# A second product by 49 multiplications, with part of its operands kept in HBM

## The chip, the core and the metric

The kernel runs on one core of a Trainium2 chip. The metric is the device time of one execution in microseconds (us). Before the change it is 684.05 us, the median of three runs from 683.75 to 684.24. The profile covers one execution of its own, with a span of 683.1 us.

## What is computed

A recurrent attention ("retention") feeds a two-layer block with a sigmoid gate. All values are fp32 (the two weight matrices arrive as float64 bits and are narrowed in the kernel).

```python
# q, k, v: (4, 8, 768, 64); w_in: (512, 2048); w_out: (2048, 512)
for t in range(S):
    state = gamma * state + k[t] (outer) v[t]        # per batch and head, 64 x 64
    y[t]  = scale * q[t] @ state
x = y, as rows of 8 heads x 64 = (3072, 512)
h = x @ w_in                                         # the first product
g = h / (1 + exp(-1.702 * h))
out = g @ w_out                                      # the second product
```

## The kernel before

The 3072 rows are worked in six blocks m = 0..5 of 512. Attention runs in chunks of 128 steps, four to a block and ahead of the products, so that the attention of block m + 1 lies inside the second product of block m. From block 2 on, both products use a seven-product scheme: the operands are seen as 2 x 2 quarters, and seven products of sums of quarters, added in the right way, give the four quarters of the result. In blocks 0 and 1 only the second product does so.

The matmuls are in the order in which the program gives them; the other engines' instructions are put in order by a scheduler when the program is compiled, and each engine, and each engine's queue of transfers, then works strictly in that order.

The loads of one attention chunk. Later chunks fetch q and k as 16 small pieces each, in the arrangement that VectorE's 32 x 32 transposes need:

```python
for name, src in (("q", q), ("k", k)):
    t = two.tile([P, HP, P // C4, C4], F32, name=name + "_sq")        # two buffers
    for r0 in range(0, P, C4):
        for n in range(P // C4):
            tc.keep_in_program_order(sp.dma_start(t[r0:r0 + C4, :, n], ...))     # 16 KB each
...
def turn(j):                                       # j: the chunk
    for t, name in ((QT[j], "q"), (KT[j], "k")):
        tc.keep_in_program_order(dve.transpose(..., QKV.pop((name, j))...))
    if 2 * CB <= j < NCH - 2:
        load(j + 2, "qk")

def step(j, f=None):                               # scores of chunk j, outputs of chunk f = j - 1
    attend(j, f)                                   # TensorE
    masked(j); decay(j)                            # VectorE; GpSimd (kd)
    ... by_state(f), output(f), aged(f), updated(f)   # VectorE and GpSimd; output writes X
    load(j + 1, "v")                               # kn and v, SyncE
```

The first product of blocks 2 to 5, for a quarter `d` of the hidden columns:

```python
def up(d):
    def product(acc, sa, sb, start, stop):
        for u in range(2):
            for c in range(2):
                pe.matmul(acc[:, u, :], W1[:, 2 * d + u, sa, c, :], X[:, sb, c, :], ...)   # 128 x 256
    ...                                            # seven products; VectorE adds, ScalarE copies and gates
    hidden(a[1], x)                                # the last of four gated quarters of G
```

The second product (quarter sums of G are made by `sums_g`, of W2 by `sums_w2` in block 0):

```python
def part(key, sa, sb, new, last, d, then):
    ...
    for p in range(2 * d, 2 * d + 2):
        for n in range(2):
            pe.matmul(p0[:, n, :], g1(m, p, sa)[:, n * P:(n + 1) * P], W2[:, sb, p, :], ...)   # 128 x 256
    if d == NP // 2 - 1:
        then(p0)
P_ = [("x", 0, 0, ...), ("y0", 1, 2, ...), ("y1", 3, 1, ...), ("x", 0, 5, ...),
      ("y2", 3, 4, ...), ("x", 2, 6, ...), ("x2", 1, 3, ...)]        # seven products, 4 units each
```

The blocks:

```python
for m in range(NB):
    between = ... chunks((m + 1) * CB + 1, (m + 2) * CB)      # turn, step, turn, step, ...
    if m > 1:
        for d in range(NP // 2):
            up(d)
    for n, unit in enumerate(down(m)):             # 28 units
        unit()
        if m == 0 ...: sums_w2, sums_w2_t3
        if m == 1 and n % 8 == 3: sums_w1(n // 4)
        if between and n % 3 == 2:
            between.pop(0)()
            if m and not between:
                sums_x()                           # GpSimd: quarter sums of X for the next first product
```

W1 and W2 lie in SBUF with their seven quarter forms, `W1[P, 8, 7, 2, 128]` and `W2[P, 7, 8, 256]`, both for the whole execution.

Of the kernel before, what the change touches and what calls it, by code (L numbers as in the profile page):

```python
# [9 lines left out]
F32 = mybir.dt.float32  # L10
U32 = mybir.dt.uint32
AF = mybir.ActivationFunctionType
ALU = mybir.AluOpType
P = 128
# [14 lines left out]
def kernel(  # L29
# [29 lines left out]
    pe, act, dve, pool, sp = nc.tensor, nc.scalar, nc.vector, nc.gpsimd, nc.sync  # L59
    ctx.enter_context(tc.manual_schedule(engines={mybir.EngineType.PE}))  # L60

    B, H, S, D = q.shape
# [3 lines left out]
    NC = S // D  # L66
    NCH = B // 2 * NC
    CB = 4
    BT = CB * P
    TH = BT // 2  # L70
    NB = NCH // CB
    NFF = DFF // P
    NP = NFF // 2
    C4 = 32
    EH = DM // 2
    assert 2 * D == P and HP * P == DM and NC % CB == 0 and B % 2 == 0 and DM == 512 and NFF == 16

    const = ctx.enter_context(tc.tile_pool(name="const", bufs=1))
    one = ctx.enter_context(tc.tile_pool(name="one", bufs=1))
    two = ctx.enter_context(tc.tile_pool(name="two", bufs=2))  # L80
    ps_a = ctx.enter_context(tc.tile_pool(name="ps_a", bufs=1, space=bass.MemoryType.PSUM))
    ps = ctx.enter_context(tc.tile_pool(name="ps", bufs=2, space=bass.MemoryType.PSUM))

# [1 line left out]

    W1 = const.tile([P, NP, 7, 2, P], F32, name="W1")
    W2 = const.tile([P, 7, NP, EH], F32, name="W2")

    X = const.tile([P, 7, 2, TH], F32, name="X")

    G = const.tile([P, NP, 4, TH], F32, name="G")
# [8 lines left out]
    mask = const.tile([P, 2, HP, D], F32, name="mask")  # L102
    state = [const.tile([P, 2, HP, D], F32, name=f"state{i}") for i in range(2)]


    ordered = [True]

    def pin(i):
        return tc.keep_in_program_order(i) if ordered[0] else i
# [47 lines left out]
    def raw(i, n=1):  # L157
        x = RAWS[i // 2 % 3]
        return x[:, i % 2 * 1024:(i % 2 + n) * 1024]
# [5 lines left out]
    class Narrow:  # L165
# [4 lines left out]
        def __init__(self, i):  # L170
            n, p, h = (1 if i < 2 else 2), i // 2 % NP, i % 2

            if i < 2:
                m = W1[:, 1, 2 * h:2 * h + 2].rearrange("p s c f -> p (s c f)")
                w = W1[:, 0, h:4:2].rearrange("p ab c f -> p c ab f")
            elif i < NFF:
                m = W1[:, p, 0:4].rearrange("p s c f -> p (s c f)")
                w = W1[:, p, 0:4].rearrange("p (ab h) c f -> p (h c) ab f", ab=2)
            else:
                m = w = W2[:, 0:4, p]  # L180
            x = raw(i, n).rearrange("p (n two) -> p n two", two=2)
            self.lo, self.hi, self.m, self.w, self.i = x[:, :, 0], x[:, :, 1], m, w, i
            if i >= NFF:
                self.lo, self.hi = [t.rearrange("p (s e) -> p s e", s=4) for t in (self.lo, self.hi)]
            self.mu = m.bitcast(U32)
# [148 lines left out]
    def step(j, f=None):  # L334
        attend(j, f)
        if j is not None:
            masked(j)
            if j > 2 * CB:
                decay(j)
        if f is not None:  # L340
            c = f % NC
            if c == 0:
                updated(f)
            else:
                by_state(f)
            output(f)
            if 0 < c < NC - 1:
                aged(f)
                updated(f)
        if j is not None and 2 * CB < j < NCH - 1:  # L350
            load(j + 1, "v")


    def hidden(g, h):

        for g, i in g if isinstance(g, list) else [(g, slice(0, 2))]:
            pin(act.activation(g, h[:, i], AF.Gelu_apprx_sigmoid))  # L357

    def g(m, p, s):

        if m:
            return G[:, p:p + 2, s, :]
        if s < 3:
            return W1[:, p:p + 2, 4 + s].rearrange("p a c f -> p a (c f)")
        return X[:, 4 + p // 2] if p < 6 else G0

    def g1(m, p, s):
        return g(m, p // 2 * 2, s)[:, p % 2]

    def up0(th, p, tag):  # L370

        h = ps.tile([P, 2, TH], F32, name="ph", tag=tag)
        for ab in range(2):
            for c in range(4):
                w = W1[:, p, 2 * ab + c // 2, c % 2, :]
                pe.matmul(h[:, ab], w, X[:, 2 * th + c // 2, c % 2, :], start=(ab == 0 and c == 0), stop=(c == 3),  # L376
                          skip_group_check=True)
        if th == 0:
            return W1[:, p, 4:6].rearrange("p s c f -> p (s c f)"), h
        return [(g1(0, p, 2 + i), i) for i in range(2)], h  # L380

    def up1(f):

        p, ab = divmod(f, 2)
        h = ps.tile([P, 2, TH], F32, name="ph", tag="xy"[f % 2])
        for c in range(4):
            w = W1[:, p, 2 * ab + c // 2, c % 2, :]
            pe.matmul(h, w, X1[:, c // 2:4:2, c % 2, :], start=(c == 0), stop=(c == 3))  # L388
        return G[:, p, ab:4:2, :], h


    def sums_w1(p):
        w = [W1[:, p:p + 2, s] for s in range(7)]
        pool.tensor_add(w[4], w[2], w[3])
        pool.tensor_sub(w[6], w[0], w[2])
        pool.tensor_sub(w[5], w[4], w[0])
        pool.tensor_sub(w[2], w[1], w[5])

    def sums_x():
        pool.tensor_sub(X[:, 4], X[:, 2], X[:, 0])  # L400
        pool.tensor_sub(X[:, 6], X[:, 3], X[:, 2])
        pool.tensor_sub(X[:, 5], X[:, 3], X[:, 4])
        pool.tensor_sub(X[:, 2], X[:, 1], X[:, 5])
# [17 lines left out]

    def up(d):

        def product(acc, sa, sb, start, stop):
            for u in range(2):
                for c in range(2):
                    pe.matmul(acc[:, u, :], W1[:, 2 * d + u, sa, c, :], X[:, sb, c, :],  # L427
                              start=(start and u == 0 and c == 0), stop=(stop and c == 1), skip_group_check=True)

        a = [G[:, 2 * d:2 * d + 2, s, :] for s in range(4)]  # L430
        x = ps.tile([P, 2, TH], F32, name="px", tag="x")
        product(x, 0, 0, True, False)
        p1 = one.tile([P, 2, TH], F32, name="p1", tag="s1")
        act.activation(p1, x, AF.Copy)
        y = ps.tile([P, 2, TH], F32, name="py1", tag="y")
        product(y, 1, 1, True, True)
        dve.tensor_add(a[0], y, p1)  # L437
        hidden(a[0], a[0])
        product(x, 5, 5, False, False)
        u = one.tile([P, 2, TH], F32, name="u", tag="s2")  # L440
        act.activation(u, x, AF.Copy)
        z = ps.tile([P, 2, TH], F32, name="py2", tag="y")
        product(z, 4, 4, True, True)
        t = one.tile([P, 2, TH], F32, name="t", tag="s1")
        dve.tensor_add(t, z, u)  # L445
        product(x, 6, 6, False, False)
        vv = one.tile([P, 2, TH], F32, name="vv", tag="s3")
        act.activation(vv, x, AF.Copy)
        y = ps.tile([P, 2, TH], F32, name="py3", tag="y")
        product(y, 2, 3, True, True)  # L450
        dve.tensor_add(a[3], z, vv)
        hidden(a[3], a[3])
        dve.tensor_add(a[2], y, t)
        hidden(a[2], a[2])
        product(x, 3, 2, False, True)
        hidden(a[1], x)

    def down(m):

# [69 lines left out]
    first = const.tile([P, 1], F32, name="first")  # L529
    idle = ps.tile([P, 4 * P], F32, name="idle", tag="x")  # L530
    works, products = {}, {}
# [62 lines left out]
    for name, i in [("0a", 0), ("0b", 1)] + [(str(p), 2 * p) for p in range(1, NFF)]:  # L594
        n = Narrow(i)
# [40 lines left out]
    def chunks(first, last):  # L636

        return [s for j in range(first, last + 1)
                for s in (lambda j=j: turn(j), lambda j=j: step(j, j - 1))]

    for m in range(NB):
        between = []
        if m == 0:
            between = [lambda: turn(2 * CB), lambda: step(2 * CB), lambda: None, lambda: None, lambda: turn(2 * CB + 1)]
        elif m == 1:
            between = [lambda: (decay(2 * CB), load(2 * CB + 1, "v"))] + chunks(2 * CB + 1, 3 * CB)[1:]
        elif 1 < m < NB - 2:
            between = chunks((m + 1) * CB + 1, (m + 2) * CB)
        elif m == NB - 2:
            between = chunks((m + 1) * CB + 1, NCH - 1) + [lambda: step(None, NCH - 1)]  # L650
        if m > 1:
            for d in range(NP // 2):
                up(d)
        for n, unit in enumerate(down(m)):
            unit()
            if m == 0 and n < NP and n % 2:
                sums_w2(n - 1)
            if m == 0 and NP <= n < 3 * NP // 2:
                sums_w2_t3(2 * (n - NP))
            if m == 1 and n % 8 == 3:  # L660
                sums_w1(n // 4)
            if between and n % 3 == 2:
                between.pop(0)()
                if m and not between:
                    sums_x()


# [44 lines left out]
```

## Time and profile before

| quantity | value |
|---|---|
| time, median of 3 | 684.05 us |
| span of the profile | 683.1 us |
| TensorE, matmuls (PE) | 671.5 us busy |
| TensorE, weight loads (PEld) | 559.3 us |
| VectorE (DVE) | 306.0 us |
| ScalarE (ACT) | 151.0 us |
| GpSimd (POOL) | 124.9 us |
| moved by transfers | 46.54 MB |
| q and k pieces after the first chunks | 512 transfers of 16 KB, issued by SyncE (SP) |
| granted TensorE clock | 1.0 |

How the profile is read. Times are microseconds from the span's start. PE holds the matmuls and PEld the weight loads of TensorE; both overlap, and a matmul's end is modelled, so a group's mean duration is longer than the distance between two starts. `L495` is a line of the kernel; `out<-in` names tiles without buffer numbers. In a group's row, the busy time and mean duration in ns stand behind the first bar, and behind the second the engine's idle time ahead of these instructions with what ended it. SPq is SyncE's queue of transfers: its rows in the timeline show how long *issuing* takes. The time from issue to landing is listed apart, as a median for each kind of transfer.

The matmuls' lines are L376 (`up0`) and L388 (`up1`) in blocks 0 and 1, L427 (`up`) from block 2 on, L495 (`part`) and L480 (last part of block 5). Attention is at L265, L275, L284 and L290, VectorE's transposes at L235, the q and k pieces at L140, kn and v at L126.

### The profile page before, as it was taken

The numbers are of one execution on the slowest core, as the hardware profiler recorded it, in microseconds if no ns is written. First come the engines' busy times: TensorE is split into PE (matmuls) and PEld (weight loads), VectorE is DVE, ScalarE is ACT, GpSimd is POOL, SyncE is SP. The second block draws the span as 40 slices with busy tenths as digits, with TensorE's granted clock in tenths as the row PEclk, the third lists the DMA queues.
The fourth block names the chain that finished last, engine by engine and source line by source line (L and its number), as shares of the span: only waits on it lengthen the run. The fifth ranks groups of instructions, "written<-read, shape, count | busy, mean of one in ns | idle before, by whom it ended". The sixth has DMA issues, their size and how long they took to land.

```text
span 683.1 us, 13807 instructions
## 1 busy us (share of the span) xinstructions
PE 671.5 (98%) x5830; PEld 559.3 (82%) x5830; DVE 306.0 (45%) x410; ACT 151.0 (22%) x301; POOL 124.9 (18%) x116
## 2 busy tenths in 40 slices
PE   7899999999999999999999999999999999999997
PEld 4788854747888888888888888888888888888886
DVE  3789881869710842221652222563222372222241
ACT  4675423321000001332000332000333000233000
POOL 3000000000467414000334100245100243000020
PEclk9999999999999999999999999999999999999999
DMA  8887641332222223301333310323310210000001
GB/s 188 215 227 222 173 141 59 123 84 35 47 33 67 59 46 88 69 6 19 72 58 76 67 23 13 72 44 78 74 35 8 59 32 32 16 0 1 16 0 46
DMA packets 140334, 46.54 MB, mean 68 GB/s; under 512 B 131825, under 2 KB 132849, under 8 KB 140273
## 3 DMA queue, kind: packets, MB, share of 16 engines
q1 hardware_dynamic: 136352, 39.10, 24.8%
q0 software_dynamic: 1760, 5.26, 2.0%
q10 hardware_dynamic: 2160, 1.31, 0.6%
q8 instruction: 45, 0.74, 0.4%
q14 instruction: 17, 0.13, 0.1%
HBM read 39.33 MB, written 6.29 MB: 67 GB/s over the span
## 4 chain that ended last, share of the span: by engine, by line
PE 87%; DVE 5%; SPq 3%; DMA 3%; issue 1%; POOL 0%; ACT 0%; ACTq 0%; DVEq 0%
PE pd L495 37%; PE px L427 16%; PE py L427 12%; PE ph L376 8%; PE ph L388 5%; SPq L140 3%; PE pt L232 2%; PE pa L265 2%; PE py L290 2%; PE py L284 1%; PE pa L275 1%; DMA whole<-in_col_decay_dram 1%; PE pd L480 1%; DMA q_in<-in_q_dram 1%; DMA W<-in_moe_w_out_dram 1%; DVE G L417 1%
## 5 line engine op out<-in xcount | busy, mean ns | idle before, releaser
L495 PE MATMUL pd<-W,G 128*128 128x256 f32 x1088 | 240.5, 381 | 0.4 <-DVE G L418 0.3
L495 PEld LDWEIGHTS pd<-W,G 128*128 128x128 f32 x1088 | 205.2, 190 | 29.4 <-DVE G L418 1.2
L427 PE MATMUL px<-X,W 128*128 128x256 f32 x512 | 119.0, 379 | 0.0
L427 PEld LDWEIGHTS px<-X,W 128*128 128x128 f32 x512 | 97.3, 190 | 13.2
L427 PE MATMUL py<-X,W 128*128 128x256 f32 x384 | 90.7, 379 | 0.0
L427 PEld LDWEIGHTS py<-X,W 128*128 128x128 f32 x384 | 73.0, 190 | 9.9
L376 PE MATMUL ph<-X,W 128*128 128x256 f32 x256 | 57.6, 382 | 0.3 <-DVE X L312 0.3
L388 PE MATMUL ph<-W,W 128*128 128x512 f32 x128 | 55.6, 592 | 0.0
L376 PEld LDWEIGHTS ph<-X,W 128*128 128x128 f32 x256 | 48.1, 190 | 8.6 <-issue 1.6
L256 POOL TENSOR_TENSOR kd<-kn_in,cold 128x512 f32<-128x512 f32 x14 | 16.3, 1167 | 199.0 <-PE pa L275 111.9
L388 PEld LDWEIGHTS ph<-W,W 128*128 128x128 f32 x128 | 24.3, 190 | 28.9 <-issue 28.7
L419 POOL TENSOR_TENSOR G<-G 128x512 f32<-128x512 f32 x20 | 28.9, 1451 | 92.9 <-DVE G L418 91.1
L357 ACT ACTIVATE G<-G 128x512 f32<-128x512 f32 x48 | 30.2, 630 | 48.5 <-DVE G L437 29.9
L437 DVE TENSOR_TENSOR G<-py,p 128x512 f32<-128x512 f32 x16 | 11.1, 692 | 66.0 <-PE py L427 66.0
L296 DVE TENSOR_TENSOR at<-pa,mask 128x512 f32<-128x512 f32 x16 | 10.9, 684 | 60.5 <-PE pa L275 60.5
L495 PE MATMUL pd<-W,W 128*128 128x256 f32 x160 | 35.8, 381 | 0.4 <-DVE W L418 0.3
L495 PEld LDWEIGHTS pd<-W,W 128*128 128x128 f32 x160 | 30.2, 190 | 5.6 <-DVE W L418 1.2
L324 POOL TENSOR_TENSOR state<-state,whole 128x512 f32<-128x512 f32 x13 | 13.7, 1057 | 114.7 <-DVE state L332 114.5
L467 ACT ACTIVATE u<-pd 128x512 f32<-128x512 f32 x6 | 3.6, 597 | 135.7 <-PE pd L495 135.7
L472 POOL DMA_DIRECT2D out_dram<-o x20 | 14.9, 745 | 93.3 <-DVE o L471 93.3
L445 DVE TENSOR_TENSOR t<-py,u 128x512 f32<-128x512 f32 x16 | 11.1, 692 | 44.0 <-PE py L427 44.0
L193 DVE TENSOR_SCALAR W<-W 128x1024 f32<-128x1024 f32 (+1 forms) x17 | 11.2, 659 | 33.4 <-ACT W L189 33.0
(109 smaller groups left out, 643.5 us busy)
## 6 DMA issues: line engine op xcount, KB each, us to landing
W<-in_moe_w_in_dram SPq DMA_DIRECT2D x12, 512.0 KB, 5.8
v_in<-in_v_dram SPq DMA_DIRECT2D x48, 128.0 KB, 3.4
kn_in<-in_k_dram SPq DMA_DIRECT2D x42, 128.0 KB, 3.2
W<-in_moe_w_out_dram SPq DMA_DIRECT2D x10, 512.0 KB, 3.7
out_dram<-o POOLq DMA_DIRECT2D x20, 256.0 KB, 2.7
q_sq<-in_q_dram SPq DMA_DIRECT2D x256, 16.0 KB, 1.9
k_sq<-in_k_dram SPq DMA_DIRECT2D x256, 16.0 KB, 1.9
G<-in_moe_w_out_dram SPq DMA_DIRECT2D x6, 512.0 KB, 4.5
```

Source lines behind the costliest of these rows:

```text
L140: tc.keep_in_program_order(sp.dma_start(t[r0:r0 + C4, :, n], src[b + n * C4 // D, h0:h0 + HP, t0:t0 + C4, d0:d0 + C4] .rearrange("h p d -> ...
L232: pe.matmul(p[n][HALF[r], s, :], x[n][:, HP * r + s, :], ident, start=True, stop=True)
L256: pool.tensor_mul(KD[j], x, d.to_broadcast([P, H, D]))
L265: pe.matmul(pa[HALF[i], r, 0, s, :], KT[j][HALF[r], s, HALF[i]], QT[j][HALF[r], s, HALF[i]], start=True, stop=True)
L324: pool.tensor_mul(new, old, whole[:, None, :, None].to_broadcast([P, 2, HP, D]))
L357: pin(act.activation(g, h[:, i], AF.Gelu_apprx_sigmoid))
L376: pe.matmul(h[:, ab], w, X[:, 2 * th + c // 2, c % 2, :], start=(ab == 0 and c == 0), stop=(c == 3), skip_group_check=True)
L388: pe.matmul(h, w, X1[:, c // 2:4:2, c % 2, :], start=(c == 0), stop=(c == 3))
L419: pool.tensor_sub(a[1], a[1], a[0])
L427: pe.matmul(acc[:, u, :], W1[:, 2 * d + u, sa, c, :], X[:, sb, c, :], start=(start and u == 0 and c == 0), stop=(stop and c == 1), skip_gr ...
L472: (pool if m < NB - 1 else act).dma_start(rows[th, e], o)
L495: pe.matmul(p0[:, n, :], g1(m, p, sa)[:, n * P:(n + 1) * P], W2[:, sb, p, :], start=(new and p == 0 and n == 0), stop=(last and p == NP - ...
```

## The change

In blocks 2 to 5 the second product applies the seven-product scheme at two levels: each of the seven outer products, on operands of half the size, is again made of seven. There are 49 products of sixteenths, each a run of four 128 x 128 x 128 matmuls, in place of seven of sixteen 128 x 128 x 256. More sums are needed: for G inside `up` (inner sums of each quarter) and in `derive`, for the outputs on GpSimd in `put`, and for W2, three further sums for each outer product.

SBUF has no room for all of W2's inner sums. They are made once in block 1 (`inner_w2`, in three of X's tiles), stored in HBM as `W2D`, and from there a ring of two places gets those of outer product i + 2 when product i is done. The ring and the operands made by `derive` (`own`) share their space with the second half of W1's forms (`W1B`), which is therefore stored in HBM too and read back ahead of each later first product. Sums of X are moved to behind the last attention step.

The core of the diff, with cuts:

```diff
-    W1 = const.tile([P, NP, 7, 2, P], F32, name="W1")
+    W1A = const.tile([P, NP // 2, 7, 2, P], F32, name="W1A")
+    W1B = [late.tile([P, 2, 7, 2, P], F32, name=f"W1B{i}", tag=f"late{i}") for i in range(2)]
+    W1D = [dram.tile([P, 2, 7, 2, P], F32, name=f"W1D{i}") for i in range(2)]
+    W2D = [dram.tile([P, 3, NP // 2, P], F32, name=f"W2D{i}") for i in range(7)]
...
 def sums_w1(p):
+        if p >= NP // 2:
+            sp.dma_start(W1D[p // 2 - 2], W1B[p // 2 - 2])
...
 def up(d):
+        for k in ((slice(0, 1), slice(2, 4), slice(1, 2)) if d == NP // 2 - 1 else (slice(0, 4),)):
+            q = [[G[:, 2 * d + i, k, h * P:(h + 1) * P] for h in range(2)] for i in range(2)]
+            dve.tensor_sub(q[0][1], q[0][0], q[0][1])
+            dve.tensor_sub(q[1][1], q[1][1], q[0][1])
+        dve.tensor_sub(a[2], a[0], a[2])
+        dve.tensor_sub(a[3], a[3], a[2])
+    ORDER = [(0, 0), (1, 2), (3, 5), (2, 6), (0, 4), (1, 3), (2, 1)]
+    def inner_w2(i):
+        b11, b12, b21, b22 = w2q(ORDER[i][1])
+        t = []
+        for k, a in enumerate((b12, b22, b21)):
+            t.append(X[:, 4 + k].rearrange("p c (d e) -> p (c d) e", e=P))
+            dve.tensor_sub(t[k], a, t[k - 1] if k else b11)
+            sp.dma_start(W2D[i][:, k], t[k])
+    def sums_g_outer(k):                           # two sums of 128 x 1024
+            if k == 0:    pool.tensor_add(a[0], a[0], a[3])
+            elif k == 1:  pool.tensor_sub(a[1], a[1], a[3])
+            else:         dve.tensor_add(a[2], a[2], a[3])
+    def down49(m):
+        ring = late.tile([P, 7, 4, P], F32, name="ring", tag="late0")
+        own = late.tile([P, 7, 4, P], F32, name="own", tag="late1")
+        def stream(i):
+            comps[i] = ring[:, i % 2 * 3:i % 2 * 3 + 3]
+            sp.dma_start(comps[i], W2D[i])
+        def derive(i):                             # three sums of 128 x 512
+            dve.tensor_add(d[:, 0], s2, a11)
+            dve.tensor_sub(d[:, 1], a12, s2)
+            dve.tensor_add(d[:, 2], s2, s3)
+            return [(a11, b11), (a12, b21), (s2, t2), (s3, t3)], [(d[:, 0], t1), (d[:, 1], b22), (d[:, 2], t4)]
+        def products(p0, pairs, new):
+            for j, (a, w) in enumerate(pairs):
+                for d in range(NP // 2):
+                    pe.matmul(p0[:, j, :], a[:, d], w[:, d], ...)          # 128 x 128
...
+        stream(0)
+        stream(1)
+        for i in range(7):
+            for half in range(2):                  # 14 units
+                    if i == 0 and half == 0: pairs[0] = derive(0)
+                    products(acc[x, half], pairs[i][half], i not in (2, 3))
+                    then(i, half, acc[x, half])    # ScalarE keeps, or VectorE puts
+                    if half == 0 and i < 6: pairs[i + 1] = derive(i + 1)
+                    if half == 1:
+                        if i + 2 < 7: stream(i + 2)
+                        if i in (0, 1, 3): sums_g_outer((0, 1, None, 2)[i])
...
         if m > 1:
+            if m > 2:
+                W1B[:] = [late.tile([P, 2, 7, 2, P], F32, ...) for i in range(2)]
+                for i in range(2):
+                    sp.dma_start(W1B[i], W1D[i])
...
-        for n, unit in enumerate(down(m)):
+        for n, unit in enumerate(down(m) if m < 2 else down49(m)):
+            if m == 1 and n % 3 == 1 and n < 21:
+                inner_w2(n // 3)
-            if between and n % 3 == 2:
+            if between and (n % 3 == 2 if m < 2 else n % 3):
                 between.pop(0)()
+            if 1 < m < NB - 1 and n == 11:
+                sums_x()
```

## The prediction

> **What bounds the kernel now.** I read the engine shares first, then the busy time by stage, then the groups, and last the timeline of SyncE's DMA issues, which decides this case.
>
> ```profile
> PE 671.5 (98%) x5830; PEld 559.3 (82%) x5830; DVE 306.0 (45%) x410; ACT 151.0 (22%) x301; POOL 124.9 (18%) x116
> ```
>
> TensorE is busy 98% of the span: only fewer or shorter matmuls, with nothing new to wait for, can shorten it. By stage (windows set by me to the second product of block 1, then the first and second products of block 2 and those of block 5; columns: PE, PEld, DVE, ACT, POOL busy, clock, DMA share, GB/s):
>
> ```profile
> 209.80:266.60 56.80, 56.80 (x706) 49.62 (x705) 26.44 (x38) 1.79 (x3) 24.23 (x22) 1.00 0.23 52
> 314.90:371.70 56.80, 56.80 (x706) 49.62 (x705) 25.32 (x37) 2.98 (x5) 19.96 (x18) 1.00 0.31 61
> 371.70:420.00 48.30, 48.30 (x226) 42.51 (x225) 12.70 (x19) 16.52 (x27) 2.37 (x3) 1.00 0.19 40
> 630.30:683.10 52.80, 48.88 (x224) 42.04 (x223) 14.24 (x18) 2.39 (x4) 5.63 (x4) 1.00 0.06 20
> ```
>
> PE has no gap before block 5's tail. A second product is 48.4 us of matmuls; in blocks 1 to 4 four attention steps of about 2.1 us lie inside it. VectorE has half of such a stage free.
>
> ```profile
> L495 PE MATMUL pd<-W,G 128*128 128x256 f32 x1088 | 240.5, 381 | 0.4 <-DVE G L418 0.3
> L495 PEld LDWEIGHTS pd<-W,G 128*128 128x128 f32 x1088 | 205.2, 190 | 29.4 <-DVE G L418 1.2
> ```
>
> A record lasts 381 ns, but records overlap: busy time over count is 240.5 / 1088 = 221 ns, and starts in a run lie 216 ns apart. Every fp32 matmul of the program is two records: all groups of the second product hold 1344 = 6 blocks x 112 x 2.
>
> ```profile
> 314.59 7.47 SPq L140 DMA_DIRECT2D q_sq<-in_q_dram  x16
> 322.16 8.49 SPq L140 DMA_DIRECT2D k_sq<-in_k_dram  x16
> 330.75 1.28 SPq L126 DMA_DIRECT2D kn_in<-in_k_dram  x2
> 332.12 1.36 SPq L126 DMA_DIRECT2D v_in<-in_v_dram  x2
> 335.07 8.49 SPq L140 DMA_DIRECT2D q_sq<-in_q_dram  x16
> 343.66 7.49 SPq L140 DMA_DIRECT2D k_sq<-in_k_dram  x16
> ```
>
> This is what to notice. Transfers move little (61 GB/s), but **issuing** them is slow: the 32 small q and k transfers of one attention chunk take SyncE 16.1 us (0.47 us each net of breaks), kn and v 2.7 more. Over blocks 2 and 3 I take 16.3 + 2.7 = 19 us a chunk. Four chunks a block make 76 us of issuing, from 314.6 to about 393; nothing waits for it now, because chunks are fetched two ahead. One more row, of SyncE's own waits, shows what releases a chunk's issue, the transposes that free the q and k buffers:
>
> ```profile
> SPq L140 <- DVE qT L235: 86.6, 6, 26.6
> ```
>
> **What the Trainium skill says.** "TensorE: Matmul & The Clock Gate", LDWEIGHTS: a load costs columns / 1.2 ns whatever the rows, 107 ns for 128. The trace agrees: where a run starts, the first load starts, the second starts 109 ns later, and the first matmul's record is 104 ns longer than the next (483 against 379). The 190 ns of a load are thus latency; its slot is 109 ns. Same page, Part 1: after about 3.4 us without work TensorE falls to half clock, and needs as long to come back. The trace has no such gap later, but its start shows the two rates: 16 transposing matmuls take 1.98 us at 6.6 us and 1.09 at 15.4 us. "DMA: Bandwidth & Descriptors", Issuing engines are not separate DMA queues: issuing elsewhere only saves sequencer time, "usually small relative to the DMA itself". For these q and k loads the trace disagrees: 0.47 us each, landed in 1.9 us and overlapping, so issue is the limit. Same page, Anatomy of one DMA: a wait happens on the issuing sequencer before dispatch. A transfer that waits thus holds back all behind it.
>
> **The change part by part.**
>
> 1. *Fewer multiplications.* 7 products of 16 matmuls of 256 columns become 49 of 4 matmuls of 128 columns: 196 x 2 records in place of 112 x 2. A 128-column stream should start every 109 ns: the trace's transposing matmuls (128 moving columns) keep 109 ns within one half of the array, and the load slot above is also 109. So 392 x 0.109 = 42.7 us against 48.4: **-5.7 us** a block, -23 us in four. This is all that can be won.
>
> 2. *VectorE and GpSimd.* Gone: 12 sums of G (0.69 to 0.97 us each) in the second product. New there: 21 sums `derive` x 0.69 = 14.5 us, two of 1024 elements, some 1.3 us each, and halves instead of wholes in the output sums. VectorE goes from 25 to about 34 us of a stage of over 51; the first product gains 16 x 0.69 = 11 us on 12.7 of 48. GpSimd gets four sums of 1024 elements (2.5 us each, twice its 1.27) and 16 short ones. Neither becomes the bound.
>
> 3. *W1's second half from HBM.* Two transfers of 1.8 MB, needed 24 and 36 us into the next first product. At the 227 GB/s of the page's best slice they take 8 us each. Hidden.
>
> 4. *The ring.* Each of the seven outer products i = 0..6 needs a 786 KB transfer, two in store. Landing, from the page's 1.9 us for 16 KB and 3.7 for 512 KB: 1.9 + 2.8 = 4.7 us. Alone it would hide behind a product of 6.1 us. But it is issued by SyncE too, and the compiled order of that queue in blocks 2 and 3 is: ring 0, 1, 2, q/k of a chunk, kn/v, ring 3, q/k, ring 4, kn/v, ring 5, q/k, kn/v, ring 6, q/k, kn/v, W1. Rings 0 to 2 wait for the first product and for i = 0, so no chunk slips ahead of them. Let 0 be the start of the second product. VectorE does the first transposes at about 8.0 (some 10 short sums ahead of them). Then:
>  - ring 3 issued at 8.0 + 16.3 + 2.7 = 27.0, lands 31.7. PE wants it at 3 x 6.1 + 2 attention steps of 2.2 + 8 matmuls (1.7) = 24.4: stall 7.3.
>  - ring 4 issued at 27.5 + 16.3 = 43.8, lands 48.5; wanted at 31.7 + 4.4 + 1.7 = 37.8: stall 10.7.
>  - ring 5 lands 51.7; wanted at 56.8: in time.
>  - ring 6 issued at 47.5 + 16.3 + 2.7 = 66.5, lands 71.2; wanted at 65.0: stall 6.2. End at 71.2 + 4.4 = 75.6.
>  Before, this stage was 56.8: **+18.8 us** in each of blocks 2 and 3. Block 4 fetches only one more chunk: one stall of 7.3, 42.7 + 8.4 + 7.3 = 58.4 against 56.4, **+2**. Block 5 has no attention: -5.7, and +1.5 for a longer last chain (half an output sum, four short sums, a whole store): **-4**.
>
> 5. *Making the ring's content in block 1.* `inner_w2` sums on VectorE into three scratch tiles, SyncE stores them, and the next set must wait for that store. The compiled order puts the stores of sets 3, 5 and 6 behind a chunk's q/k loads, and puts VectorE's waiting sums ahead of the next transposes and masks, which attention on PE needs. One turn of this loop: q/k 16.3 + issue 0.5 + landing 2.7 (256 KB row) + three sums 2.1 + two transposes 1.4 = 23.0 us. PE has 10.4 + 2.1 = 12.5 us of work in that time, so it stalls 10.5 us, in two turns; the store of 1.8 MB ahead of set 2 should cost about 2 more before them. **+23 us**.
>
> Sum of the chains: 23 + 2 x 18.8 + 2 - 4 = +58.6, thus 743 us. Two terms that I can only estimate: TensorE's half clock after stalls of 7 to 11 us, about 2 us where PE sets the end (blocks 1 to 4: +8), and the ring's packets ahead of the small ones, which hold SyncE up when it waits for earlier loads (+3 in blocks 2 and 3: +6). I predict **755 us**.
>
> **The rivals.** *(a) The multiplication gain arrives.* If small transfers were issued faster, or landing alone counted, rings would arrive in time and the result be near 684 - 23 + 3 = 664. For it: DMA share of 0.31 and 1.9 us landings. Against: the 0.47 us stand in every chunk of the timeline with transfers idle. *(b) VectorE becomes the bound*, through GpSimd's locks and order: the sums of G cost 0.69 us alone and up to 1.75 beside GpSimd. If all 34 us grew by half, 51 us would just fill the stage: about 684 +/- 5. Against: its work is spread over the stage. *(c) 128-column matmuls run slower than 109 ns*, because load and stream now fill the same slot. At 130 ns a product takes 51 us: +8 us a block, less where it hides in the ring's stalls; from my 755 some 770, from (a)'s 664 some 697. Against: the 109 ns between the first two loads. *(d) Only the ring or only block 1 stalls*, if VectorE runs ahead more than I think: 684 - 23 + 3 + 28 (block 1 with clock, no ring) = 692, or 755 - 25 = 730.
>
> **Range and chances.** The issue chain carries the answer; for it to vanish the compiled order would have to be harmless in two separate places. The lower end, 727, is close to case (d) with stalls in the blocks only; the upper, 783, doubles the estimated terms and takes part of (c). Faster than 2% needs (a) whole: 0.04. Within 2%: 0.05. Slower: 0.91.
>
> **What would show it.** Step 1: starts of `pq` matmuls 109 ns apart in a run; 42.7 us of them in block 5. Step 4: PE idle ended by DMA into the ring three times in each of blocks 2 and 3 and once in block 4, 6 to 11 us each, with q/k issues just before the ring's in SyncE's timeline; ring landings near 4.7 us. Step 5: in block 1, PE waits for transposed q and k twice for about 10 us while VectorE waits for stores of W2's sums. Clock: below 1.00 after those gaps. PE's busy share should fall under 90%. I am wrong if SyncE's issue runs ahead of the rings, if a ring lands later than 6 us for bandwidth, or if VectorE, not a DMA, ends PE's waits in the second product.

## The result and the profile after

The changed kernel takes **769.48 us**, median of 4 (768.91 to 771.12), against 683.9 us (681.91 to 684.24) for the kernel before beside it: a ratio of 1.126, interval 1.123 to 1.129. The profiled execution has a span of 767.5 us.

From the page after: the shares of the engines and the granted clock in 40 slices.

```profile
PE 673.7 (88%) x6502; PEld 585.5 (76%) x6502; DVE 439.4 (57%) x597; ACT 156.7 (20%) x313; POOL 190.0 (25%) x164
...
PEclk9999999999999879999787999987799997999999
```

TensorE is no longer busy all the time, though it has more records (6502 for 5830); the clock dips in four places, one for each of blocks 1 to 4. By stage (columns as before: busy times of PE, PEld, DVE, ACT, POOL, clock, DMA share, GB/s), for the second product of block 1, the second product of block 2, the next first product, and block 5:

```profile
209.80:286.20 76.40, 58.32 (x698) 50.84 (x697) 46.22 (x61) 1.79 (x3) 27.77 (x22) 0.89 0.55 163
334.50:421.00 86.50, 60.52 (x880) 58.74 (x880) 45.94 (x62) 5.72 (x10) 38.16 (x33) 0.84 0.39 96
421.00:469.50 48.50, 48.50 (x230) 42.80 (x229) 20.50 (x31) 16.30 (x27) 2.35 (x4) 1.00 0.37 130
713.00:767.50 54.50, 47.25 (x407) 46.48 (x406) 35.87 (x57) 5.47 (x10) 13.21 (x4) 0.99 0.27 93
```

The first product is as it was: 48.5 us, all of it PE. Block 2's second product has 26 us without PE. Neither VectorE nor GpSimd fills a stage; in block 2's second product VectorE works 45.9 of the 86.5 us. What PE waited for (columns: us in total, times, longest):

```profile
PE pq L541 <- DMA ring<-W2D: 57.2, 7, 9.7
PE pa L275 <- DVE kT L245: 20.4, 5, 9.5
```

Seven waits for the ring, and two long ones (of five) for the transposed k. SyncE's timeline (start, duration of the issues) tells why the ring is late:

```profile
343.76 9.01 SPq L149 DMA_DIRECT2D q_sq<-in_q_dram  x16
352.88 8.41 SPq L149 DMA_DIRECT2D k_sq<-in_k_dram  x16
361.70 1.31 SPq L135 DMA_DIRECT2D kn_in<-in_k_dram  x2
363.12 1.27 SPq L135 DMA_DIRECT2D v_in<-in_v_dram  x2
364.49 0.57 SPq L525 DMA_DIRECT2D ring<-W2D  x1
365.16 8.31 SPq L149 DMA_DIRECT2D q_sq<-in_q_dram  x16
373.56 8.60 SPq L149 DMA_DIRECT2D k_sq<-in_k_dram  x16
382.25 0.38 SPq L525 DMA_DIRECT2D ring<-W2D  x1
```

PE's last start ahead of ring 3 is at 361.97. The ring is issued at 364.49, behind 17.5 us of q and k and 2.7 of kn and v, and PE's next start is at 369.38. For ring 4 the three times are 377.87, 382.25 and 386.82. (A single wait is told here from start to start, and so holds the matmul ahead of it; the rows of waits leave that out and are 0.3 to 0.4 us shorter.) Issue of the ring itself is short, and so is its landing (last number, median us from issue to landing):

```profile
ring<-W2D SPq DMA_DIRECT2D x28, 768.0 KB, 4.8
```

In block 1, VectorE waits for a store and only then transposes q and k; PE, whose last start was at 246.62, goes on at 254.86:

```profile
251.32 0.69 DVE L495 TENSOR_TENSOR X<-W 128x512 f32<-128x512 f32 x1 [6.92 <-DMA W2D<-X]
...
254.05 0.67 DVE L245 STREAM_TRANSPOSE kT<-k_sq 128x512 f32<-128x512 f32 x1
```

### The profile page after: what moved, and what is told of

It reads as the page before. It is cut to its first block, busy times and chain, and to the rows that moved or that the text cites. A ratio compares the mean times of both kernels' runs of the same rounds, so it can differ in the third digit from the quotient of the medians.

```text
span 767.5 us, 15539 instructions
## 1 busy us (share of the span) xinstructions
PE 673.7 (88%) x6502; PEld 585.5 (76%) x6502; DVE 439.4 (57%) x597; ACT 156.7 (20%) x313; POOL 190.0 (25%) x164
## 4 chain that ended last, share of the span: by engine, by line
PE 63%; SPq 13%; DMA 10%; DVE 9%; issue 3%; POOL 1%; ACT 0%; ACTq 0%; DVEq 0%; POOLq 0%
PE pq L541 17%; PE px L445 14%; PE py L445 11%; SPq L149 10%; PE ph L388 7%; DMA ring<-W2D 6%; PE ph L401 4%; PE pd L655 4%; PE pt L242 2%; SPq L135 2%; DMA W2D<-X 2%; PE pa L275 2%; DVE X L495 1%; PE pa L285 1%; PE py L294 1%
## 5 line engine op out<-in xcount | busy, mean ns | idle before, releaser
L541 PE MATMUL pq<-W,G 128*128 128x128 f32 x672 | 90.2, 287 | 2.3 <-ACT own L579 2.3
L541 PEld LDWEIGHTS pq<-W,G 128*128 128x128 f32 x672 | 85.3, 203 | 3.0 <-ACT own L579 2.5
L541 PE MATMUL pq<-ring,G 128*128 128x128 f32 x224 | 36.7, 317 | 57.2 <-DMA ring<-W2D 57.2
L541 PEld LDWEIGHTS pq<-ring,G 128*128 128x128 f32 x224 | 32.9, 226 | 58.6 <-DMA ring<-W2D 58.6
L508 POOL TENSOR_TENSOR G<-G 128x1024 f32<-128x1024 f32 x8 | 27.8, 3494 | 197.9 <-DVE own L533 197.9
L541 PE MATMUL pq<-ring,own 128*128 128x128 f32 x448 | 62.2, 284 | 0.0
L445 PE MATMUL px<-X,W1A 128*128 128x256 f32 x256 | 59.8, 379 | 0.0
L445 PE MATMUL px<-X,W1B 128*128 128x256 f32 x256 | 59.8, 379 | 0.0
L541 PEld LDWEIGHTS pq<-ring,own 128*128 128x128 f32 x448 | 56.8, 199 | 0.5
L445 PEld LDWEIGHTS px<-X,W1B 128*128 128x128 f32 x256 | 48.7, 190 | 6.6
L445 PEld LDWEIGHTS px<-X,W1A 128*128 128x128 f32 x256 | 48.5, 190 | 6.4
L655 PE MATMUL pd<-W,G 128*128 128x256 f32 x224 | 50.2, 383 | 0.8 <-DVE G L434 0.8
L655 PEld LDWEIGHTS pd<-W,G 128*128 128x128 f32 x224 | 42.5, 192 | 7.0 <-DVE G L434 1.2
```

The source lines that it names most:

```text
L445: pe.matmul(acc[:, u, :], t[:, q1 + u, sa, c, :], X[:, sb, c, :], start=(start and u == 0 and c == 0), stop=(stop and c == 1), skip_group_ ...
L508: pool.tensor_add(a[0], a[0], a[3])
L541: pe.matmul(p0[:, j, :], a[:, d], w[:, d], start=(new and j == 0 and d == 0), stop=(d == NP // 2 - 1), skip_group_check=True)
```

## The experiments

The theory: all of the loss is the order in which transfers, and instructions that wait, stand in the queue that issues them. Rivals: the ring's bandwidth, VectorE's extra sums, the shorter matmuls. Each run changes who issues a transfer or where an instruction stands; the arithmetic and the output stay. The table gives the median time and, from the one profiled execution of each, the lengths of the stages that move (us): second products of blocks 0 and 1 together, then second (S) and first (F) products by block. Three profiled executions lie away from their median: 731.4 us (ring and stores on ScalarE), 711.9 (the same, stores moved) and 678.3 (four waits taken away). Small differences to these rows mean little. Block 5 runs to the start of its last matmul. The first product of block 2 is 48.3 or 48.4, that of block 5 48.3 or 48.4, in all.

| kernel | time | S 0+1 | S 2 | F 3 | S 3 | F 4 | S 4 | S 5 |
|---|---|---|---|---|---|---|---|---|
| before | 683.9 | 106.8 | 56.8 | 48.3 | 57.2 | 48.3 | 56.3 | 49.1 |
| changed | 769.5 | 128.3 | 84.6 | 48.3 | 86.6 | 48.3 | 62.8 | 46.2 |
| ring, W1 reload on ScalarE | 732.7 | 129.8 | 66.6 | 58.1 | 67.8 | 48.3 | 54.4 | 47.8 |
| stores on ScalarE | 758.9 | 116.0 | 85.6 | 48.3 | 87.0 | 48.3 | 63.3 | 46.2 |
| ring, W1 reload and stores on ScalarE | 727.1 | 116.1 | 65.4 | 57.3 | 65.6 | 57.8 | 57.9 | 47.9 |
| some k on ScalarE | 749.9 | 127.2 | 78.3 | 48.3 | 78.0 | 48.3 | 61.1 | 46.3 |
| ring on ScalarE, early turn | 721.8 | 129.4 | 60.8 | 56.6 | 62.1 | 53.3 | 51.7 | 47.9 |
| the same, stores moved | 707.2 | 117.8 | 61.6 | 56.3 | 60.4 | 53.4 | 51.7 | 47.7 |
| four waits taken away | 684.7 | 111.4 | 53.9 | 51.8 | 54.8 | 50.7 | 51.7 | 43.7 |
| the same, one k on ScalarE | 687.8 | 111.1 | 58.1 | 54.5 | 59.7 | 49.0 | 51.7 | 43.7 |
| the same as four, first rings on GpSimd | 676.1 | 112.6 | 53.2 | 48.3 | 55.5 | 48.3 | 51.7 | 43.7 |

**The ring on ScalarE.**

```diff
-            sp.dma_start(comps[i], W2D[i])
+            act.dma_start(comps[i], W2D[i])
-                    sp.dma_start(W1B[i], W1D[i])
+                    act.dma_start(W1B[i], W1D[i])
```

> The ring's transfers and the re-reading of W1's second half are issued by ScalarE instead of SyncE; nothing else changes. If SyncE's issuing of q and k pieces ahead of them is the cause (theory), PE's waits for the ring vanish: the second products of blocks 2 and 3 fall from 85 and 87 us to about 52, that of block 4 from 63 to about 52, block 1 stays at +21 us: 692 us (682 to 702). If the ring is late for bandwidth or landing time, hardly any change: above 755. If VectorE's added sums are the bound behind it, PE's waits are then for VectorE: 715 to 745.

Measured: 732.74 us, ratio 1.072 (1.066 to 1.078). PE's waits in this kernel:

```profile
PE pa L275 <- DVE kT L245: 38.4, 7, 9.5
PE px L445 <- ACT p L452: 7.3, 1, 7.3
```

No wait for the ring is left, and its landing is as before (4.7 us): the order of issue was the cause of the seven waits. But only 37 of the 77 expected us came back, and the waits have new names. Two lines of VectorE, and one of ScalarE, show why:

```profile
378.42 0.71 DVE L245 STREAM_TRANSPOSE qT<-q_sq 128x512 f32<-128x512 f32 x1 [0.73 <-DMA k_sq<-in_k_dram]
...
388.81 0.71 DVE L245 STREAM_TRANSPOSE kT<-k_sq 128x512 f32<-128x512 f32 x1 [9.67 <-DMA v_in<-in_v_dram]
```

```profile
402.87 9.93 ACTq L815 DMA_DIRECT2D W1B<-W1D  x2
412.84 0.60 ACT L452 ACTIVATE p<-px 128x512 f32<-128x512 f32 x1 [46.39 <-DMA k_sq<-in_k_dram]
```

The fourth chunk of a stage can be fetched only after the second has been turned in the same stage (at 355.88), and its q and k queue behind the third's: they were issued from 365.87 to 384.46, the slowest k piece landed 5.2 us after its issue, and kT starts at 388.81. (The releaser named is a load of v, but its two transfers went out at 385.9 and 386.6 and took 3.4 us or more; they landed later than that.) So the chunk chain is itself a second limit, which the ring's stalls had covered. And ScalarE, holding W1's reload, reaches the copy `p` only at 412.84, while PE has waited since 405.86.

**The stores on ScalarE**, and **both together**.

```diff
-            sp.dma_start(W1D[p // 2 - 2], W1B[p // 2 - 2])
+            act.dma_start(W1D[p // 2 - 2], W1B[p // 2 - 2])
-            sp.dma_start(W2D[i][:, k], t[k])
+            act.dma_start(W2D[i][:, k], t[k])
```

> Only the stores of block 1 (W2's inner sums and W1's second half) are issued by ScalarE; the ring stays on SyncE. Theory: the two waits of PE for transposed q and k (8.2 and 9.9 us) vanish and block 1 comes back to within 5 us of its 56.8: 752 us (746 to 758), with the seven ring waits unchanged. If block 1 is slower because VectorE has 28 more sums there: 764 to 771.

Measured: 758.86 us, ratio 1.110 (1.105 to 1.115). Block 1 falls by 12.3 us and keeps 9.2, where at most 5 were expected; the rest stays:

```profile
PE pq L541 <- DMA ring<-W2D: 58.5, 7, 9.5
PE pa L275 <- DVE kT L245: 9.7, 4, 6.6
```

One gap of 7.0 us is left in block 1, again while VectorE waits for W2's stores. The two losses are independent places of the same cause.

> Both at once: every added transfer is issued by ScalarE. Theory: what is left is the gain of the multiplications, 4 x (48.4 - 43.9) = 18 us by the 112 ns seen between starts, less 1.4 for the tail, some 4 in block 1 and up to 2 for each second product in waits for VectorE: 676 us (664 to 690), so about the time before or a little under. If bandwidth is the cause: above 745. If VectorE is: 695 to 730.

Measured: 727.13 us, the median of four from 715.10 to 731.37. Two of the four took over 1.5% longer than the fastest; the ratio, 1.053 (1.043 to 1.064), is of the other two, whose mean of 720.2 is 44 us above what was expected. Added to the ring's move, that of the stores brings 6 us by the medians and 12.5 by these two. The profiled execution, the longest, shows both parts: 13.7 us less in block 1, but 9.4 more in block 4's first product, where PE waits behind W1's reload on ScalarE once more, and 3.5 more in its second.

**The k pieces of later chunks on ScalarE**, with the ring on SyncE: half of what stands ahead of a ring.

```diff
-                        tc.keep_in_program_order(sp.dma_start(
+                        tc.keep_in_program_order((act if name == "k" and j > 14 else sp).dma_start(
```

> The ring stays on SyncE. From block 2 on the k pieces (half of the small transfers) are issued by ScalarE, so that a chunk takes SyncE 8 us less. Theory: rings 3, 4 and 6 are issued 8, 16 and 24 us sooner and land in time; ScalarE's copies wait up to 8 us behind its own issues, which costs PE some 5 us in blocks 2 and 3: 700 us (688 to 715). If the place or size of the ring's transfers is at fault and not what stands ahead of them: 760 to 775.

Measured: 749.89 us, ratio 1.096 (1.089 to 1.103); PE waits 42.1 us for the ring in place of 57.2. In block 2 the stalls are 5.3, 5.5 and 9.4 us for 7.4, 8.95 and 9.85. Fewer issues ahead do shorten a stall; the last hardly moved. The expectation of 700 was far off.

**The ring on ScalarE and an earlier first turn**, against the second limit. W1's reload goes back to SyncE.

```diff
-            sp.dma_start(comps[i], W2D[i])
+            act.dma_start(comps[i], W2D[i])
...
                 up(d)
+                if d == 1 and between:
+                    between.pop(0)()
```

> The ring's transfers are issued by ScalarE; W1's reload and all stores stay on SyncE; and the first turn of each next block (its transposes, which release the fetch of the chunk two further on) is given out in the first product, after quarter d = 1, so that the fetch starts some 25 us earlier. Theory: two limits lie one behind the other in SyncE's queue, first the order (ring behind q and k), then the length of the chunk chain from the first turn on. With both gone, no wait for the ring and none for transposed q and k in blocks 2 and 3: second products of blocks 2, 3 and 4 at about 53 us (44 of matmuls, four attention steps of 2.1), against 84.6, 86.6 and 62.8 of the changed kernel less some. Block 1 stays at +21. Total 690 to 700. Rival: the kernel is held by the ring's bandwidth or by VectorE; then waits of several us stay in blocks 2 and 3 and it is 720 or more, as when only the ring was moved (733).

Measured: 721.77 us, ratio 1.056 (1.051 to 1.060). Block 1 still has its two gaps (the first row), and blocks 2 and 3 came down to 61 and 62 us, not 53:

```profile
PE pa L275 <- DVE kT L245: 17.9, 2, 9.0
PE pq L541 <- DVE o L562: 12.2, 2, 6.5
PE px L445 <- DMA W1B<-W1D: 8.6, 2, 5.5
```

**The same with the stores moved.**

```diff
-            sp.dma_start(W2D[i][:, k], t[k])
+            act.dma_start(W2D[i][:, k], t[k])
-            sp.dma_start(W1D[p // 2 - 2], W1B[p // 2 - 2])          # in sums_w1
...
+            for i in range(2 if m == 2 else 0):                     # at the start of block 2
+                sp.dma_start(W1D[i], W1B[i])
```

> As the kernel with the earlier first turn and the ring on ScalarE, and the stores of W2's inner sums are issued by ScalarE too, with W1's stores taken out of block 1's way to the start of block 2's first product. Theory: block 1's loss was the stores' place behind q and k and behind W1's 3.6 MB; it falls from +21 to 2 to 5 us. Total 672 to 680, the gain of the multiplications less the longer tail and what block 1 keeps. Rival: VectorE's extra sums in block 1 are the loss; then block 1 keeps 9 us or more, as when only the stores were moved, and the total is 685 or more.

Measured: 707.20 us, ratio 1.035 (1.032 to 1.038). Three kinds of wait, 28 us in PE's list, and the half clock behind them make up the 30 us above the expectation. First, the scheduler put W1's 3.6 MB back into block 1 (issued at 217.90), and W2's stores landed behind them: VectorE waits, and PE stands for 8.8 us. Block 1 keeps 11.0 us, which by the expectation's own measure speaks for the rival, VectorE's sums; but VectorE stands idle for 6.7 us there, until a store of W2's sums has landed, and with W1's stores held back, in the next kernel, 4.6 remain. Second, the last turn of a block stands in VectorE's order ahead of a sum that frees PE's accumulator:

```profile
366.83 0.71 DVE L245 STREAM_TRANSPOSE kT<-k_sq 128x512 f32<-128x512 f32 x1 [8.46 <-DMA v_in<-in_v_dram]
...
369.36 0.68 DVE L560 TENSOR_TENSOR o<-pq,ring 128x512 f32<-128x512 f32 x1
```

PE goes on at 370.19. The k pieces of this chunk were issued from 351.80 to 362.05, a mean of 0.64 us each: most still stand 0.47 apart, but the issue pauses twice for 1.7 us. In the window from 350 to 368 us they landed later than the page's median of 2.0 us (last number):

```profile
ring<-W2D ACTq DMA_DIRECT2D x2, 768.0 KB, 5.6
k_sq<-in_k_dram SPq DMA_DIRECT2D x16, 16.0 KB, 3.1
```

This is no single case. In each of the ten kernels with the ring, after 300 us, pieces that SyncE issued while a transfer of the ring or of W1 was under way landed in 3.7 to 4.6 us (medians), the others in 1.8 to 2.0. So the large transfers go with a later landing of the small ones, from the same queue (3.9 us in the changed kernel) and from another. Third, W1's reload stands on SyncE behind all four chunks, issued at 406.81, and PE waits 7.9 us in two first products.

**Four waits taken away** from the kernel just told, one in each of four stages, so that each can be read from its own stage.

```diff
-            (act if last else pool).dma_start(rows[th, e], ...)     # block 5's stores
+            (sp if last else pool).dma_start(rows[th, e], ...)
-                    sp.dma_start(W1B[i], W1D[i])
+                    pool.dma_start(W1B[i], W1D[i])
-                sp.dma_start(W1D[i], W1B[i])
+                tc.keep_in_program_order(sp.dma_start(W1D[i], W1B[i]))
-            if between and (n % 3 == 2 if m < 2 else n % 3):
+            if between and (n % 3 == 2 if m < 2 else n in (1, 2, 4, 5, 7, 10, 11)):
...                                                                 # sums_x at n == 12
```

> As the kernel with ring and stores on ScalarE and the earlier first turn, with four further changes, each against a wait that its trace still shows: block 5's output stores on SyncE instead of ScalarE (they stand in ScalarE's order ahead of the copy that PE waits for: 2.6 us, and some 1.6 of half clock after it); W1's reload issued by GpSimd (2.5 and 4.7 us of waits in two blocks); W1's stores held in place behind block 1's last q and k loads (8.8 us of wait in block 1 and its half clock, some 10); the last turn of each block two units later (6 us twice and half clock, together some 15). Theory, all losses come from the order in which transfers and waits stand in the issuing queues: 707 - 4 - 8 - 9 - 10 = about 676. Rival, the transfers' bandwidth or the slowed issue of q and k (0.65 us each beside the ring) is the limit: the waits only move, and it stays above 695.

Measured: 684.70 us (678.28 to 688.83), ratio 1.000 (0.998 to 1.002). All four stages answered: block 5 went from 47.7 to 43.7, blocks 2 and 3 from 61.6 and 60.4 to 53.9 and 54.8, blocks 0 and 1 from 117.8 to 111.4, the two first products from 56.3 and 53.4 to 51.8 and 50.7. The median is still 9 us over the expectation. The profiled execution was the shortest of the 22, the one compared with the longest of six; the last kernel of the table, profiled close to its median, has every second product within 1.2 us of these.

**The same, with the one chunk fetched and used within a stage split between SyncE and ScalarE.**

```diff
-                        tc.keep_in_program_order(sp.dma_start(
+                        tc.keep_in_program_order((act if name == "k" and j > 12 and j % 4 == 0 else sp).dma_start(
```

> As the other kernel of this pair, and the k pieces of the one chunk that is fetched and used within the same second product (chunk 16, and 20) are issued by ScalarE. If the length of that chunk's issue (20 us on one engine) still sets the end of blocks 2 and 3, this is 4 to 8 us faster than the other, some 670; if not, it is the same within 2 us, or a little slower where ScalarE's copies wait behind 16 more issues.

Measured: 687.75 us, ratio 1.005 (1.003 to 1.006): 3 us slower by the medians of 22. The gain of 4 to 8 us is not there, so with the turn moved back that chunk's issue no longer sets the end. PE waits 5.6 us for the ring in the profiled execution (2.8 in the shortest one without the split): in block 2 ring 3 is issued by ScalarE at 338.77, behind 16 k pieces that take from 324.88 to 338.68.

**The first two rings of blocks 3 to 5 on GpSimd**, from the kernel with four waits taken away.

```diff
-            act.dma_start(comps[i], W2D[i])
+            (pool if i < 2 and m > 2 else act).dma_start(comps[i], W2D[i])
```

> As the first kernel of the last pair (ring and stores on ScalarE, earlier first turn, W1's reload on GpSimd), with the first two ring transfers of blocks 3, 4 and 5 issued by GpSimd: they wait for W1's second half to come free and stood in ScalarE's order ahead of the copies and gates of the first product, which PE then waited for (3.5 and 2.4 us in two first products). Theory: these 5 to 6 us go, and the kernel is at 677 to 680, faster than the kernel before by about 1%. Rival: the waits move to GpSimd's sums and nothing is won: 684.

Measured: **676.05 us** (675.40 to 678.82), ratio **0.990** (0.988 to 0.993) to the kernel before: both first products are back at 48.3 us. This version is 1% faster than the kernel before, clear of the noise, and 12% faster than the changed one. Its page and its longest waits:

```profile
PE 655.9 (97%) x6502; PEld 568.3 (84%) x6502; DVE 440.1 (65%) x597; ACT 156.6 (23%) x313; POOL 199.4 (30%) x176
```

```profile
PE idle L704 <- POOL ident masks.py:199: 3.9, 1, 3.9
PE pd L653 <- DVE G L432: 2.2, 1, 2.2
PE pq L539 <- DMA ring<-W2D: 2.1, 4, 0.8
PE pt L242 <- DMA q_in<-in_q_dram: 1.8, 2, 1.5
PE pa L275 <- DVE kT L245: 1.5, 1, 1.5
```

It has the same 6502 records, the same sums and the same bytes as the changed kernel, which takes 93 us more. That gap is the order of transfers and of instructions on the engines' queues, and the clock lost behind the waits. Against before, the stages give -3.6, -1.7, -4.6 and -5.4 in blocks 2 to 5 (-15.3) and +5.8 in blocks 0 and 1. Nearly all of the 5.8 lies in block 1: PE waits for VectorE 1.5 us (kT) and 2.2 us (a sum of G), and behind the second wait six starts are 427 ns apart instead of 216. VectorE works without a break from 224.93 until after both, so in this last piece its added sums are a limit.

## Why the prediction was right, point by point

The time, 769.48 us, lies in the range; it is 14 us over the 755. (The prediction's own terms add up to 684 + 58.6 + 8 + 6 = 757.) Set against the chains with their estimated terms, blocks 2 and 3 took 9.7 us more, blocks 4 and 5 2.5 each, and block 1 3.5 less.

- **Step 1, fewer multiplications: right.** Starts of `pq` are 112 ns apart for the most part, not 109, so 392 records take 43.9 us, not 42.7. Block 5, once its stores no longer held ScalarE, ran in 43.7 against 49.1: -5.4 where -5.7 was predicted. Of rival (c), slower short matmuls, 1.2 us a block came true.
- **Step 2, VectorE and GpSimd: right** in that neither bounds a stage of the changed kernel, but both under-sized. VectorE took 45.9 us of block 2's second product where I had 34; single sums of 0.69 us stretched to 2.8. GpSimd's sums of 1024 elements took 3494 and 2771 ns (means of two groups) where I had 2.5 us.
- **Step 3, W1's reload: right here.** No first product waits for it (landing 9.8 us, not 8). It is hidden only because its place in the queue happens to be early enough; in the faster versions it was not.
- **Step 4, the ring: right in each place.** Stalls in block 2 and block 3: ring 3, 7.4 and 8.1 us (7.3 predicted); ring 4, 9.0 and 9.9 (10.7); ring 5, none (none); ring 6, 9.9 and 7.7 (6.2); block 4, 7.2 (7.3). The hit on ring 3 is partly luck: the first transposes came at 5.8 us instead of 8.0, and the issue ahead of the ring took 20.7 us instead of 19.0. The mis-sized term is "+18.8 us in each of blocks 2 and 3", with 5 us of clock and SyncE held up: 23.8, measured 27.8 and 29.4. The stalls are 26.2 and 25.7 us where 24.2 were predicted, the matmuls 1.2 more; most of the rest is clock. In block 2, 84.6 - 43.9 of matmuls - 8.4 of four attention steps - 26.2 of stalls leaves 6.1, and 5.6 of that is half clock (below).
- **The rivals.** (a), the gain of the multiplications, did not arrive by itself; with the order mended, by many moves, it came in part: 676. (b) and (d) are out for the changed kernel: VectorE ended none of the long waits of blocks 2 and 3, and both places stalled.
- **The half clock: too small.** I put 2 us to each of blocks 1 to 4. Behind the seven ring stalls 132 distances between `pq` starts lie between 150 and 400 ns, nearly all at 213 instead of 112, 13 to 27 behind each stall. Together they cost 14.4 us (5.6, 6.1 and 2.7 in blocks 2, 3 and 4), thus 2 for each stall, not for each block.
- **SyncE held up: right in kind.** A chunk's q and k took 16.7 to 19.0 us in block 2, not 16.3.
- **Step 5, block 1: right.** Two waits of 8.2 and 9.9 us for kT (10.5 each predicted), VectorE waiting for W2's stores; 21.5 us in all, where 23 and 2 of clock were predicted. Moving the stores took 12.3 us of it away.
- **Block 4 and block 5: +6.5 and -1.5** where +2 (+2 of clock) and -4 were predicted. Block 4's one stall was sized right (7.2 us). Block 5's miss is a wait that I didn't see: its output store is issued by ScalarE, in order, ahead of a copy that PE needs (2.6 us; in the versions with the ring on ScalarE half clock followed it, in the changed kernel it did not). Moving that store, with three other moves in other stages, showed it: the stage fell from 47.7 to 43.7, where the changed kernel has 46.2.

What failed were my expectations of the repairs. I took each wait away as if nothing stood behind it, and was some 20 to 50 us too low in five of the first six runs; the sixth, the stores alone, missed by 7. A stall hides every wait that would have ended earlier. What stays open: why the issue of q and k pieces pauses beside the ring (the traces show that it does, and that the pieces land later, not what in the queue makes it).

## What to carry to other kernels

A queue that issues transfers is an engine with a busy time: count its issues before giving it another transfer with a deadline, and look at what stands ahead in its compiled order, not at bandwidth alone. An instruction that waits holds up all behind it on that engine, whether it is a store issue on ScalarE ahead of a copy or a transpose on VectorE ahead of a sum that frees an accumulator; here, moving such instructions to another engine or to another place in the order was worth 93 us, and the arithmetic saved some 15. And a repair is to be sized from the next wait behind the one removed.

## What the runs showed of the hardware

- fp32 matmuls of 128 moving columns start every 112 ns, those of 256 every 216, so halving the width costs about 4%. In both, each matmul record has one record of a weight load (5830 of each before, 6502 after).
- After stalls of 7 to 10 us, 13 to 27 starts were for the most part 213 ns apart instead of 112 (132 by seven stalls), about 2 us of loss a stall.
- In the changed kernel, issue on SyncE takes 0.3 to 1.4 us for a ring transfer of 786 KB (median 0.36), and pieces of 16 KB are mostly issued 0.47 us apart: bytes hardly matter. Pieces issued while a transfer of the ring or of W1 was under way landed in 3.9 us instead of 1.8 (medians). Beside the ring issued by ScalarE, one chunk's k pieces took a mean of 0.64 us each to issue, by two pauses of 1.7 us, and landed in 3.1 us.
